# First keys of the next batch before the channel table, wide scores reordered, first norms on GpSimd

## The chip, the core and the metric

The kernel runs on one core of a Trainium2 chip. Its engines are TensorE (matmul and transpose), VectorE and ScalarE (elementwise work), GpSimd (elementwise work too) and SyncE, which here only issues DMAs. Each engine runs its own instructions in order, and engines wait for each other through semaphores. The metric is the device time of one execution in microseconds (us). Times inside an execution come from a profiled one, whose span is 833.5 us; they count from the start of that span.

## The reference

```python
def _attn_ref(q, k, v):                       # (4, 8, 768, 64)
    k_sum = k.reshape(B, H, nb, 32, D).max(axis=3)      # one key per block of 32
    v_sum = v.reshape(B, H, nb, 32, D).mean(axis=3)
    scores_l = q @ k^T / sqrt(D), kept where |i - j| < 16
    scores_s = q @ k_sum^T / sqrt(D) + log(32)
    a = softmax over both together
    return a @ [v, v_sum]

def _moe_ref(x, w_ch1, w_ch2):                # x: (4, 768, 512)
    X = np.fft.fft(np.fft.fft(x, axis=1), axis=2)
    u = x + np.real(X)
    un = (u - mean(u)) / sqrt(var(u) + 1e-06)           # over the 512 channels
    return u + np.maximum(un @ w_ch1, 0) @ w_ch2        # 512 -> 2048 -> 512
```

Four batches pass through a local attention, a real 2-D Fourier mix, a norm and a two-layer product. The weights come as 64-bit floats and are converted on the chip while the first batch is worked on ("words" in the code and the profile).

## The kernel before

The first batch's attention is written in "wide" form, two heads of a pair at a time, in four pairs (`NP = 4`); later batches use another form, which is interleaved with the dense work of the batch before by a scheduler. In the opening, the order on TensorE and VectorE is the program's own order; the DMA order is the program's too.

```python
def block_sums(b, gg):                # sums of the values over blocks of 32, for four heads
    ...
    for i in range(4):
        fetch(out=raw[i], in_=src[:, n * i:n * (i + 1)])
    add = gtt if done_weights else tt         # GpSimd once the weights are done, VectorE before
    add(raw[0], raw[0], raw[1], ADD)
    add(raw[2], raw[2], raw[3], ADD)
    add(raw[0], raw[0], raw[2], ADD)
    if not done_weights:
        nc.vector.tensor_reduce(out=vb, in_=raw[0]..., op=ADD, axis=AX.X)
    ...

def wide_scores(b, g, between=None):
    for half in range(2):
        n0, n1 = ...
        ps = [abank([P, NQ // 2, QB], ...) for e in range(2)]
        for n in range(n0, n1):
            for e in range(2):                # near keys
                nc.tensor.matmul(ps[e][0:WK, n - n0, :], kt[rows, ...], qt[rows, ...])
        for e in range(2):                    # block maxima of the keys, from VectorE
            nc.tensor.matmul(ps[e][WK:P], km[rows, :], qt[rows, QB * n0:QB * n1])
        for e in range(2):
            nc.scalar.activation(out=p[:, e, n0:n1], in_=ps[e], func=AF.Exp, scale=SC)
            tt(p[:, e, n0:n1], p[:, e, n0:n1], wide[...], ALU.mult)      # mask
        if half == 0 and between:
            between()                         # the value sums of the first or second four heads

def first_attention():
    p = {0: wide_scores(0, 0, lambda: add_blocks(0))}
    prepare(0, 1)                             # transposes of queries and keys, maxima km
    sum_values(0, 0)
    load(0, 3)
    for g in range(NP - 1):
        p[g + 1] = wide_scores(0, g + 1, (lambda: add_blocks(1)) if g == 1 else None)
        wide_values(0, g, p[g], x)            # av: weights times values, reciprocal, product
        load_values(*following(0, g, 2))
        for par in range(2):
            fold_sequence(par, g)             # even and odd halves for the Fourier step
        if g == 0:
            get_tables(0)                     # fs (sequence tables) and fd (channel table)
        if g < NP - 2:
            prepare(0, g + 2)
            sum_values(0, g + 1)
        if g == NP - 3:
            load_raw(1)                       # a piece of the weights
            load(1, 0)                        # keys and queries of the next batch
            load_raw(2)
            sum_values(0, g + 2)
    fold_halves(0, 0)
    wide_values(0, NP - 1, p[NP - 1], x)
    ...                                       # the last fold steps

def gen_fourier(b):
    ...   # y: product with fs;  mx: product with fd, added to x;  then the norm, per half
        y, z = norm[:, 0], norm[:, 1]
        if b == 0:
            nc.vector.tensor_scalar(out=minus, in0=both[:, :, 0], scalar1=-1.0, ...)
            nc.vector.tensor_scalar(out=var, in0=both[:, :, 1], scalar1=1e-6, ...)
        ...
        nc.vector.tensor_scalar(out=y (int32), in0=var (int32), scalar1=1, op0=arith_shift_right)
        nc.vector.tensor_scalar(out=y (int32), in0=y, scalar1=-1.0, scalar2=float(0x5F3759DF), ...)
        for _ in range(3):                    # Newton steps for 1/sqrt
            nc.vector.scalar_tensor_tensor(out=z, in0=y, scalar=-0.5, in1=y, op0=mult, op1=mult)
            tt(z, z, var, ALU.mult)
            nc.vector.scalar_tensor_tensor(out=y, in0=z, scalar=1.5, in1=y, op0=ADD, op1=mult)
        ins = nc.vector.tensor_tensor(out=z, in0=minus, in1=y, op=mult)
    ...   # un = x * y + z (VectorE and ScalarE), transposed by TensorE (unt) and copied to u,
          # then four sums of u; the hidden layer (hx, hy, hz) reads u

block_sums(1, 0)                              # after first_attention: values of the next batch
```

Of the kernel before, what the change touches and what calls it, by code (L numbers as in the profile page):

```python
# [487 lines left out]
def _main_program(ctx, tc, q, k, v, moe_w_ch1, moe_w_ch2, out):  # L488
# [95 lines left out]

    def add_blocks(gg):
        raw, vb = to_add[gg]
        n = BLOCK * D // 2
        while n > D:
            tt(raw[:, 0:n], raw[:, 0:n], raw[:, n:2 * n], ADD)
            n //= 2  # L590
        tt(vb, raw[:, 0:D], raw[:, D:2 * D], ADD)

    def block_sums(b, gg):

        heads, rows = slice(4 * gg, 4 * gg + 4), 4 * nb
        f = BLOCK // 4
        n = f * D
        vb = spool.tile([rows, D], FP, tag="vbs", bufs=2, name=f"vbs_{b}_{gg}")
        for g in (2 * gg, 2 * gg + 1):
            sums[b, g] = vb, sel[:, g % 2]  # L600
        src = v[b, heads].rearrange("h (n f) d -> (h n) (f d)", f=BLOCK)
        if b == 0:

            raw = words[0:rows, 4 * n * gg:4 * n * (gg + 1)]
            fetch(out=raw, in_=src)
            to_add[gg] = raw, vb
            return
        if done_weights:
            raw = room(f"vb_{b}_{gg}")
            raw = [raw[0:rows, n * i:n * (i + 1)] for i in range(4)]  # L610
        else:

            raw = [bpool.tile([P, NC, P], FP, tag="s", bufs=5, name=f"vb_{b}_{gg}_{i}").rearrange("p n t -> p (n t)")
                   [0:rows] for i in range(4)]
        for i in range(4):
            fetch(out=raw[i], in_=src[:, n * i:n * (i + 1)])

        add = gtt if done_weights else tt
        add(raw[0], raw[0], raw[1], ADD)
        add(raw[2], raw[2], raw[3], ADD)  # L620
        add(raw[0], raw[0], raw[2], ADD)
        if not done_weights:
            nc.vector.tensor_reduce(out=vb, in_=raw[0].rearrange("p (f d) -> p d f", d=D), op=ADD, axis=AX.X)
        else:
            while f > 2:
                f //= 2
                gtt(raw[0][:, 0:f * D], raw[0][:, 0:f * D], raw[0][:, f * D:2 * f * D], ADD)
            gtt(vb, raw[0][:, 0:D], raw[0][:, D:2 * D], ADD)

# [72 lines left out]
    def wide_scores(b, g, between=None):  # L704

        kt, km, qt = kt_bufs[g % 2], km_bufs[g % 2], nat[b, g]
        p = apool.tile([P, 2, NQ, QB], FP, tag="p", name=f"p_{b}_{g}")
        for half in range(2):
            n0, n1 = NQ // 2 * half, NQ // 2 * (half + 1)
            ps = [abank([P, NQ // 2, QB], f"sc_{b}_{g}_{half}_{e}") for e in range(2)]  # L710
            for n in range(n0, n1):
                for e in range(2):
                    rows = slice(D * e, D * (e + 1))
                    nc.tensor.matmul(ps[e][0:WK, n - n0, :], kt[rows, QB * n:QB * n + WK],
                                     qt[rows, QB * n:QB * (n + 1)], start=True, stop=True)
            for e in range(2):
                rows = slice(D * e, D * (e + 1))
                nc.tensor.matmul(ps[e][WK:P], km[rows, :], qt[rows, QB * n0:QB * n1], start=True, stop=True)
            for e in range(2):
                nc.scalar.activation(out=p[:, e, n0:n1], in_=ps[e], func=AF.Exp, scale=SC)  # L720
                tt(p[:, e, n0:n1], p[:, e, n0:n1], wide[:, None, :].to_broadcast([P, NQ // 2, QB]), ALU.mult)
            if half == 0 and between:
                between()
        return p

    def sum_values(b, g):

        ps = abank([P, 2, D], f"vs_{b}_{g}")
        for e in range(2):
            vb, pick = sums[b, g]  # L730
            nc.tensor.matmul(ps[WK:P, e], pick[:, D * e:D * e + 32], vb, start=True, stop=True)

        (nc.vector.tensor_copy if g in (0, NP - 1) else nc.scalar.copy)(
            out=wide_vw(g)[WK:P, :, :, 0:D], in_=ps[WK:P, :, None, :].to_broadcast([P - WK, 2, NQ, D]))

    def wide_values(b, g, p, x):
        vw = wide_vw(g)
        av = [abank([P, NST, D1], f"av_{b}_{g}_{e}") for e in range(2)]
        for n in range(NQ):
            for e in range(2):  # L740
                nc.tensor.matmul(av[e][QB * (n % 2):QB * (n % 2 + 1), n // 2, :], p[:, e, n, :], vw[:, e, n, :],
                                       start=True, stop=True)
        for e in range(2):
            rc = rec[:, b * NP + g, e]
            nc.vector.reciprocal(out=rc, in_=av[e][:, :, D])
            tt(x[:, :, P * g + D * e:P * g + D * (e + 1)], av[e][:, :, 0:D],
               rc[:, :, None].to_broadcast([P, NST, D]), ALU.mult)
# [63 lines left out]
    def first_attention():  # L811

        x = x_of[0] = bpool.tile([P, NST, DM], FP, tag="x", bufs=2, name="x_0")
        fold = bpool.tile([P, 7, 2, S2], FP, tag="u", name="fold_0").rearrange("p a k n -> p (a k n)")
        wt["fold"] = fold[:, 0:3 * HT * DM].rearrange("p (i t d) -> p i t d", i=3, t=HT)
        p = {0: wide_scores(0, 0, lambda: add_blocks(0))}
        prepare(0, 1)
# [4 lines that stand above are left out]
            wide_values(0, g, p[g], x)  # L822
            load_values(*following(0, g, 2))
            for par in range(2):
                fold_sequence(par, g)
            if g == 0:
                get_tables(0)
            if g < NP - 2:
                prepare(0, g + 2)
                sum_values(0, g + 1)  # L830
            if g == NP - 3:
                load_raw(1)
                load(1, 0)
                load_raw(2)
                sum_values(0, g + 2)
        fold_halves(0, 0)
        wide_values(0, NP - 1, p[NP - 1], x)
        for par in range(2):
            fold_sequence(par, NP - 1)
            if par:  # L840
                fold_halves(par, 0)
            fold_halves(par, 1)
            fold_ends(0, par, wt["fold"][:, par], wt["fold"][:, 2 - 2 * par])
# [160 lines left out]
    def get_tables(b):  # L1004
        tag, bufs = ("w1", 3) if b else ("w2", NC)
        fs = []
        for par in range(2):
            t = bpool.tile([P, 2, HT, F2 + 1], FP, tag=tag, bufs=bufs, name=f"fs_{b}_{par}")
            fetch(out=t, in_=dr["fs"].ap()[par])
            fs.append(t)  # L1010
        if b:
            fd = bpool.tile([P, C["fm"].shape[1]], FP, tag=tag, bufs=bufs, name=f"fm_{b}")
            fetch(out=fd, in_=dr["fm"].ap())
        else:
            fd = bpool.tile([P, 6, HD], FP, tag=tag, bufs=bufs, name=f"fd_{b}")
            fetch(out=fd, in_=dr["fd"].ap())
        tables[b] = fs, fd
        return fs, fd

    def mix_halves(ps, y, fm, xt, half):  # L1020

# [16 lines left out]
    def gen_fourier(b):  # L1038
        x = x_of[b]
        Q = DM // 4  # L1040
        fs, fd = tables[b] if b in tables else get_tables(b)


        bank = abank if b else dense_bank
# [40 lines left out]
        for half in range(2):  # L1085
# [5 lines left out]
            for i in range(HT):  # L1091
# [23 lines left out]
                                     accum_out=var[:, i:i + 1])  # L1115
                yield

            y, z = norm[:, 0], norm[:, 1]
            if b == 0:
                nc.vector.tensor_scalar(out=minus, in0=both[:, :, 0], scalar1=-1.0, scalar2=None, op0=ALU.mult)  # L1120
                nc.vector.tensor_scalar(out=var, in0=both[:, :, 1], scalar1=1e-6, scalar2=None, op0=ADD)
            else:
                nc.vector.tensor_scalar(out=var, in0=var, scalar1=1.0 / DM, scalar2=1e-6, op0=ALU.mult, op1=ADD)
            nc.vector.tensor_scalar(out=y.bitcast(I32), in0=var.bitcast(I32), scalar1=1, scalar2=None,
                                    op0=ALU.arith_shift_right)
            nc.vector.tensor_scalar(out=y.bitcast(I32), in0=y.bitcast(I32), scalar1=-1.0, scalar2=float(0x5F3759DF),
                                    op0=ALU.mult, op1=ADD)
            for _ in range(3):
                nc.vector.scalar_tensor_tensor(out=z, in0=y, scalar=-0.5, in1=y, op0=ALU.mult, op1=ALU.mult)
                tt(z, z, var, ALU.mult)  # L1130
                nc.vector.scalar_tensor_tensor(out=y, in0=z, scalar=1.5, in1=y, op0=ADD, op1=ALU.mult)
            ins = nc.vector.tensor_tensor(out=z, in0=minus, in1=y, op=ALU.mult)
            if b == 0:
                marks["mx", 0] = ins.ins
            norms.append((y, z))
# [191 lines left out]
    nc.vector.memset(vs, 0.0)  # L1327
    nc.vector.tensor_scalar(out=vs[:, :, D], in0=half_of, scalar1=float(BLOCK), scalar2=None, op0=ALU.mult)

    block_sums(1, 0)  # L1330

    def second_attention():
        prepare(1, 0)
# [76 lines left out]
```

## Time and profile before

| | |
|---|---|
| time, median of 3 runs | 838.29 us (837.83 to 839.15) |
| span of the profiled execution | 833.5 us |
| TensorE busy | 803.7 us (96%), 6074 matmuls |
| VectorE busy | 487.5 us (58%), 1117 instructions |
| ScalarE busy | 254.9 us (31%) |
| GpSimd busy | 16.1 us (2%), 27 instructions |
| moved by DMA | 120.55 MB, mean 145 GB/s |

In the profile, a row of the timeline has its start and length in us, the engine, the line of the kernel, the operation, what it writes and reads, the shape and the count; square brackets give how long the engine had been idle and what ended that. `PE` is TensorE, `DVE` VectorE, `ACT` ScalarE, `POOL` GpSimd, `SPq` the queue in which SyncE issues DMAs. A row of waits has the total, the number and the longest. A matmul of 32-bit floats is recorded several times. Line 562 is a helper for elementwise operations, so the names of the tiles tell which one is meant.

### The profile page before, as it was taken

The numbers are of one execution on the slowest core, as the hardware profiler recorded it, in microseconds if no ns is written. First come the engines' busy times: TensorE is split into PE (matmuls) and PEld (weight loads), VectorE is DVE, ScalarE is ACT, GpSimd is POOL, SyncE is SP. The second block draws the span as 40 slices with busy tenths as digits, with TensorE's granted clock in tenths as the row PEclk, the third lists the DMA queues.
The fourth block names the chain that finished last, engine by engine and source line by source line (L and its number), as shares of the span: only waits on it lengthen the run. The fifth ranks groups of instructions, "written<-read, shape, count | busy, mean of one in ns | idle before, by whom it ended". The sixth has DMA issues, their size and how long they took to land.

```text
span 833.5 us, 14698 instructions
## 1 busy us (share of the span) xinstructions
PE 803.7 (96%) x6074; PEld 577.3 (69%) x6074; DVE 487.5 (58%) x1117; ACT 254.9 (31%) x561; POOL 16.1 (2%) x27
## 2 busy tenths in 40 slices
PE   8978998999999999999999999999999999999997
PEld 5757655445578855886568875787667875786586
DVE  5778998977978553543376823542357833532351
ACT  3543756444635023203234213121323502101200
POOL 0010000000000200020000000000000000000000
PEclk9989999999999999999999999999999999999999
DMA  9997697978733277247443253423312235205001
GB/s 227 216 252 146 193 246 253 289 244 259 241 108 110 83 268 200 83 77 254 101 92 103 82 208 122 127 38 131 121 46 89 71 108 209 89 1 220 1 26 54
DMA packets 101612, 120.55 MB, mean 145 GB/s; under 512 B 50560, under 2 KB 83552, under 8 KB 101344
## 3 DMA queue, kind: packets, MB, share of 16 engines
q1 hardware_dynamic: 100848, 119.31, 48.6%
q8 instruction: 50, 0.82, 0.4%
q10 hardware_dynamic: 688, 0.20, 0.1%
q14 instruction: 26, 0.21, 0.1%
HBM read 96.96 MB, written 22.54 MB: 143 GB/s over the span
## 4 chain that ended last, share of the span: by engine, by line
PE 83%; DVE 10%; ACT 3%; issue 1%; DMA 1%; ACTq 0%; DVEq 0%
PE hx L1173 18%; PE ox L1237 17%; PE hz L1173 9%; PE oz L1237 8%; PE y L1072 4%; PE o L1214 4%; PE hy L1173 4%; PE oy L1237 4%; PE mx L1029 2%; PE sc L757 2%; DVE x L562 1%; PE unt L1151 1%; PE y L1076 1%; ACT qt L696 1%; PE av L790 1%
## 5 line engine op out<-in xcount | busy, mean ns | idle before, releaser
L1173 PE MATMUL hx<-u,w 128*128 128x384 f32 x512 | 186.2, 491 | 7.2 <-DVE h L562 3.3
L1173 PEld LDWEIGHTS hx<-u,w 128*128 128x128 f32 x512 | 94.5, 190 | 72.1 <-DVE h L562 7.0
L1173 PE MATMUL hz<-u,w 128*128 128x384 f32 x256 | 93.3, 487 | 0.0
L1237 PE MATMUL ox<-w,s 128*128 128x256 f32 x336 | 81.5, 381 | 0.3
L1237 PE MATMUL oz<-w,s 128*128 128x256 f32 x336 | 80.7, 379 | 0.0
L1237 PE MATMUL ox<-w,h 128*128 128x256 f32 x336 | 78.4, 381 | 0.4 <-DVE x L562 0.4
L1173 PEld LDWEIGHTS hz<-u,w 128*128 128x128 f32 x256 | 48.4, 190 | 34.3 <-ACT h L1190 1.1
L562 DVE TENSOR_TENSOR x<-ox,x 128x256 f32<-128x256 f32 x84 | 35.3, 421 | 62.1 <-PE ox L1237 62.0
L1237 PEld LDWEIGHTS ox<-w,h 128*128 128x128 f32 x336 | 63.2, 190 | 11.1 <-DVE x L562 1.5
L1237 PEld LDWEIGHTS oz<-w,s 128*128 128x128 f32 x336 | 63.5, 190 | 8.4
L1237 PEld LDWEIGHTS ox<-w,s 128*128 128x128 f32 x336 | 62.5, 190 | 9.2 <-DVE x L562 1.1
L562 DVE TENSOR_TENSOR h<-hx,h 128x384 f32<-128x384 f32 x32 | 17.7, 555 | 67.4 <-PE hx L1173 67.4
L1183 ACT COPY h<-hx 128x384 f32<-128x384 f32 x32 | 15.3, 477 | 127.3 <-PE hx L1173 115.6
L562 DVE TENSOR_TENSOR h<-hy,h 128x384 f32<-128x384 f32 x32 | 17.8, 556 | 60.6 <-PE hy L1173 57.4
L1173 PE MATMUL hy<-u,w 128*128 128x384 f32 x128 | 46.6, 487 | 0.0
L1214 PE MATMUL o<-w,h 128*128 128x512 f32 x96 | 42.6, 596 | 1.2 <-DVE w L562 1.2
L1237 PE MATMUL oy<-w,h 128*128 128x256 f32 x168 | 39.8, 379 | 0.0
L1199 ACT ACTIVATE h<-hx 128x384 f32<-128x384 f32 x32 | 15.7, 489 | 78.7 <-PE hx L1173 78.6
L1072 PE MATMUL y<-fs,fold 128*128 128x193 f32 x192 | 37.9, 344 | 0.1
L1072 PEld LDWEIGHTS y<-fs,fold 128*128 128x128 f32 x192 | 32.1, 195 | 6.3 <-issue 4.9
L1173 PEld LDWEIGHTS hy<-u,w 128*128 128x128 f32 x128 | 24.2, 190 | 17.1 <-DVE w L562 0.6
L1237 PEld LDWEIGHTS oy<-w,h 128*128 128x128 f32 x168 | 31.9, 190 | 4.3
(141 smaller groups left out, 1073.2 us busy)
## 6 DMA issues: line engine op xcount, KB each, us to landing
w<-dw SPq DMA_DIRECT2D x44, 896.0 KB, 5.1
words<-in_moe_w_ch_dram SPq DMA_DIRECT2D x32, 512.0 KB, 6.6
dw<-w SPq DMA_DIRECT2D x12, 896.0 KB, 6.8
vw<-in_v_dram SPq DMA_DIRECT2D x47, 192.0 KB, 5.2
kn<-in_k_dram SPq DMA_DIRECT2D x16, 384.0 KB, 4.5
qn<-in_q_dram SPq DMA_DIRECT2D x16, 384.0 KB, 5.1
out_dram<-x SPq DMA_DIRECT2D x24, 256.0 KB, 2.0
fs<-c_fs SPq DMA_DIRECT2D x8, 579.0 KB, 3.5
```

Source lines behind the costliest of these rows:

```text
L562: nc.vector.tensor_tensor(out=out, in0=in0, in1=in1, op=op)
L696: nc.scalar.copy(out=dst[D * e:D * (e + 1), s:S:2], in_=ps[D * s:D * (s + 1)])
L757: nc.tensor.matmul(ps[h][r:r + 64, i, :], kt[rows, o:o + 64], qt[rows, o:o + BLOCK], start=True, stop=True)
L790: nc.tensor.matmul(av[r][32 * j:32 * (j + 1), t, :], p[rows, h, i - NB2 * h, :], vw[rows, i, :], start=(t == 0), stop=False, skip_group_ch ...
L1029: nc.tensor.matmul(out, y[:, g], table, start=True, stop=last, skip_group_check=True)
L1072: nc.tensor.matmul(y, fgs[par][:, st, P * g:P * (g + 1)], fs[par][:, g % 2, st, :], start=(st == 0), stop=(st == HT - 1))
L1076: nc.tensor.matmul(ps[0:1, par:par + F2 + 1], zq[:, par, s2:s2 + 1], fs[par][:, 0, s2, :], start=False, stop=False, skip_group_check=True)
L1173: nc.tensor.matmul(ps, w[:, a, kk, :], u[:, r, kk, :], start=start and kk == 0, stop=stop and kk == 1, skip_group_check=True)
L1183: nc.scalar.copy(out=c11, in_=X)
L1199: nc.scalar.activation(out=c21, in_=X, func=AF.Relu)
L1214: nc.tensor.matmul(ps, h[:, n, hf, P * t:P * (t + 1)], wt[2, b, j][:, 2 * hf:2 * hf + 2, :], start=(n, hf) == (0, 0), stop=(n, hf) == (NC ...
L1237: nc.tensor.matmul(ps, left[a][:, n, :], wt[2, b, j][:, r, :], start=start and n == 0, stop=stop and n == NC - 1, skip_group_check=True)
```

## The change

It has four parts. The next batch's first keys and queries, two pieces of the weights and the values for the next batch's block sums are loaded ahead of the channel table, which is wanted only after y; the additions of those values are called apart from their load, and end in two additions instead of a reduce. The wide scores do the near keys of both halves before the key maxima of either, so that TensorE has work while VectorE makes the maxima; they use all four attention banks of PSUM at once, and the values move to the other four banks. The first batch's norms run on GpSimd, but for the shift, to leave VectorE to other work. For this a Newton step is written with four simple instructions instead of three, which holds for the later batches' norms on VectorE too.

```diff
     def add_blocks(gg):
         raw, vb = to_add[gg]
-        n = BLOCK * D // 2
-        while n > D:
-            tt(raw[:, 0:n], raw[:, 0:n], raw[:, n:2 * n], ADD)
+        n = BLOCK * D
+        add = gtt if done_weights else tt
+        if isinstance(raw, list):
+            add(raw[0], raw[0], raw[1], ADD)
+            add(raw[2], raw[2], raw[3], ADD)
+            add(raw[0], raw[0], raw[2], ADD)
+            raw, n = raw[0], n // 4
+        while n > 2 * D:
             n //= 2
-        tt(vb, raw[:, 0:D], raw[:, D:2 * D], ADD)
+            add(raw[:, 0:n], raw[:, 0:n], raw[:, n:2 * n], ADD)
+        add(vb, raw[:, 0:D], raw[:, D:2 * D], ADD)
...
-    def block_sums(b, gg):
+    def block_sums(b, gg, now=True):
...                                  # the additions go out of it
+        to_add[2] = raw, vb
+        if now:
+            add_blocks(2)
...                                  # wide_scores
+        ps = [[abank([P, NQ // 2, QB], ...) for e in range(2)] for half in range(2)]
+        for n in range(NQ):
+            half, i = divmod(n, NQ // 2)
+            for e in range(2):
+                nc.tensor.matmul(ps[half][e][0:WK, i, :], kt[rows, ...], qt[rows, ...])
         for half in range(2):
-            ps = [abank(...) for e in range(2)]
-            for n in range(n0, n1):
-                for e in range(2):
-                    nc.tensor.matmul(ps[e][0:WK, n - n0, :], kt[rows, ...], qt[rows, ...])
             for e in range(2):
-                nc.tensor.matmul(ps[e][WK:P], km[rows, :], qt[rows, QB * n0:QB * n1])
+                nc.tensor.matmul(ps[half][e][WK:P], km[rows, :], qt[rows, QB * n0:QB * n1])
...                                  # sum_values, wide_values
-        ps = abank([P, 2, D], f"vs_{b}_{g}")
+        ps = bank([P, 2, D], f"vs_{b}_{g}")
-        av = [abank([P, NST, D1], f"av_{b}_{g}_{e}") for e in range(2)]
+        av = [bank([P, NST, D1], f"av_{b}_{g}_{e}") for e in range(2)]
...                                  # first_attention; get_tables(0) no longer loads fd
             if g == 0:
                 get_tables(0)
+            elif g == 1:
+                load(1, 0)
+                load_raw(2)
+                block_sums(1, 0, False)
+                get_channel_table(0)
...
             if g == NP - 3:
-                load_raw(1)
-                load(1, 0)
-                load_raw(2)
                 sum_values(0, g + 2)
...                                  # gen_fourier
+            eng = nc.vector if b else nc.gpsimd
...                                  # the scalings, the step and the last product: eng
             for _ in range(3):
-                nc.vector.scalar_tensor_tensor(out=z, in0=y, scalar=-0.5, in1=y, op0=mult, op1=mult)
-                tt(z, z, var, ALU.mult)
-                nc.vector.scalar_tensor_tensor(out=y, in0=z, scalar=1.5, in1=y, op0=ADD, op1=mult)
+                eng.tensor_tensor(out=z, in0=y, in1=y, op=ALU.mult)
+                eng.tensor_tensor(out=z, in0=z, in1=var, op=ALU.mult)
+                eng.tensor_scalar(out=z, in0=z, scalar1=-0.5, scalar2=1.5, op0=mult, op1=ADD)
+                eng.tensor_tensor(out=y, in0=y, in1=z, op=ALU.mult)
...
-    block_sums(1, 0)
+    add_blocks(2)
```

The scheduler that orders the dense stages answers to these durations. In the changed program, three of the first batch's transposes of un stand on TensorE before the first values product of the next batch's attention, and the other three after its first sixth; VectorE adds the new block sums right after the folds; and in later batches one or two matmuls of the batch before move ahead of the transposes of un.

## The prediction

> **What bounds the kernel now.** I read the busy slices of the page first, then the table of stages, then the timeline of the stages where TensorE is not full, and last the waits.
>
> ```profile
> ## 2 busy tenths in 40 slices
> PE   8978998999999999999999999999999999999997
> DVE  5778998977978553543376823542357833532351
> PEclk9989999999999999999999999999999999999999
> ```
>
> Each digit is 20.8 us. TensorE is full nearly everywhere, VectorE only in the first ten slices. The table of stages (columns: TensorE, weight loads, VectorE, ScalarE, GpSimd busy us with counts, granted clock, DMA share, GB/s) says how much TensorE leaves idle in each:
>
> ```profile
> 0.00:52.00 52.00, 41.68 (x642) 31.35 (x642) 36.51 (x83) 21.30 (x42) 2.80 (x13) 0.97 0.99 224
> 52.00:75.50 23.50, 23.50 (x111) 18.81 (x110) 15.83 (x39) 7.34 (x22) 1.97 (x3) 0.91 0.95 208
> 75.50:91.00 15.50, 12.97 (x346) 10.87 (x346) 14.68 (x52) 11.52 (x21) 0.00 (x0) 0.89 0.63 164
> 91.00:130.00 39.00, 34.96 (x321) 21.19 (x321) 38.76 (x80) 25.75 (x52) 0.00 (x0) 1.00 0.86 230
> 200.00:834.00 634.00, 621.78 (x4173) 459.52 (x4171) 321.69 (x745) 156.75 (x369) 11.30 (x12) 1.00 0.37 118
> ```
>
> 10.3 us idle before 52, none from 52 to 75.5, 2.5 to 91, 4.0 to 130 with VectorE full, 12.2 spread over the last 634. The change touches little after 130 us, so it plays for the first three gaps, 16.8 us, of which most belongs to work it leaves alone. Behind 130 TensorE is a queue: what it gains earlier arrives at the end unshortened.
>
> The end of the opening, in the timeline:
>
> ```profile
> 42.05 0.50 SPq L549 DMA_DIRECT2D kn<-in_k_dram  x1
> 42.59 0.54 SPq L549 DMA_DIRECT2D qn<-in_q_dram  x1
> 47.47 0.85 PE L694 MATMUL qk<-ident,kn 128*128 128x128 f32 x6 [3.02 <-DMA kn<-in_k_dram]
> 49.62 0.55 DVE L873 TENSOR_TENSOR fold<-fold 128x381 f32<-128x381 f32 x1
> 49.74 1.51 PE L694 MATMUL qk<-ident,qn 128*128 128x128 f32 x6 [1.42 <-DVE fold L562]
> 51.77 0.42 PE L757 MATMUL sc<-qt,kt 64*64 64x32 f32 x2 [0.52 <-ACT qt L696]
> 52.12 2.94 PE L1072 MATMUL y<-fs,fold 128*128 128x193 f32 x8
> ```
>
> The first Fourier product y stands in TensorE's queue behind the transposes of the next batch's first keys and queries and two score matmuls. Those keys were issued at 42.05 and landed 5.3 us later; the queries took 7.0 us from 42.59, to 49.6, which is when their transposes start (the release named, a fold step, only comes last by a hair). y's own input, the even half of the fold, is ready at 50.17. So the next batch's load costs y 1.95 us.
>
> Further on, TensorE's waits from 75 to 130 us:
>
> ```profile
> PE hx L1173 <- DVE h L562: 2.3, 1, 2.3
> PE vs L780 <- DVE norm L1126: 1.8, 1, 1.8
> ```
>
> The second is really the sums of values (a reduce that ends at 81.0), which queue on VectorE between the Newton steps. The first norms take VectorE from 73.95 to 86.33: 28 instructions of 0.15 us, 4.2 us, stretched because each step of three numbers per partition waits its turn behind 0.7 us instructions.
>
> **What the Trainium skill says.** GPSIMD Engine Reference, 3.1 Elementwise — side-by-side cycle accounting: about 2.6 cycles an element for two inputs plus a software dispatch per instruction. Three elements are all dispatch. The trace has such sizes, by form:
>
> ```profile
> L868 POOL COPY zq<-fold 128x3 f32<-128x3 f32 x2 | 1.0, 490 | 2.3 <-DVE fold L562 2.3
> L565 POOL TENSOR_TENSOR vbs<-vb 96x64 f32<-96x64 f32 x2 | 0.6, 316 | 128.9 <-PE vs L780 128.9
> L1294 POOL COPY vw<-wide 128x24 f32<-128x24 f32 x2 | 0.4, 228 | 5.1 <-DMA wide<-c_count 5.1
> ```
>
> A 128x24 copy beside an idle VectorE takes 0.23 us, a 128x3 copy beside VectorE's adds 0.49. That agrees with SBUF — State Buffer, Who interferes with whom: a VectorE instruction with two SBUF inputs and a GpSimd instruction that reads SBUF exclude each other; one 128x6 copy here lasted 1.33 us beside such adds (51.70). TensorE: Matmul & The Clock Gate, Part 1: The HAM clock gate, says that an idle window of about 3.4 us halves the clock and a busy one restores it. The trace agrees: the clock reads 0.50 from about 49.4 to 56.0, after the thin stretch from 44.5, and again from 83.4 to 86.4 after the wait at 79.3. So a gap removed or made costs up to 1.7 us besides itself.
>
> **Part 1, wide scores.** No instruction is added; per head pair the 24 near-key matmuls of the second half (1.24 us) go ahead of the key-maximum ones (0.8). For pair 0 that fills TensorE's 1.5 us wait for the maximum, for nothing: VectorE is full and its order is kept. For pair 1 the first half's scores come 1.24 us later, VectorE starts its mask about 0.65 us later (20.4 for 19.76), but the 1.16 us it waits before the second half vanishes. I walked the queues forward with durations from the timeline (near keys 1.23 a half, maxima 0.77, av 1.6, transposes 2.62, mask pair 1.03): av of pair 0 ends at 22.2 for 22.99; pair 2's first mask starts at 29.0 for 28.53 (a loss); pair 3's second mask ends at 40.9 for 41.73. All that follows on VectorE moves 0.85 us: even fold ready at 49.3. The values now share four PSUM banks with the transposes; I find waits of 0.15 us there and neglect them.
>
> **Part 2, load order.** Ahead of the keys stood the channel table (768 KB) and one 512 KB piece of weights. From 31.7 to 49.6 the queue moved about 3.85 MB, some 0.22 to 0.24 MB per us; 1.3 MB less is 5.5 us. Keys land near 42, queries near 44.5, transposes run at once after the last av (42.6), eight ScalarE copies of 0.52 us end by 49, eight score matmuls follow by 49.2. y then starts at 49.4 instead of 52.12: **2.7 us**, of which 0.85 are part 1's. The table is wanted at 62.5; issued near 48, with 7.9 us to landing before, it comes in time. The value sums move into VectorE's 4.9 us wait at 55.7 (four loads landed by about 53), so their 3.0 us leave the tight stretch.
>
> **Part 3, norms on GpSimd.** Per half: two scalings, one shift that stays on VectorE, one step, three Newton rounds of four, one product: 14 dependent GpSimd instructions after the shift. At 0.23 to 0.32 plus 0.08 between (from the chain of value adds on GpSimd), with some blocking, 0.35 each: 4.9 us. Statistics of half one are ready at 70.8 (73.45 less 2.7). GpSimd scalings and shift end at 71.6, the norm at 76.5 against 81.68. Then half two, whose statistics stand behind the first normalised block on VectorE, starts at 77.2 and ends at 82.6 against 86.33. So the left factor u is complete some 4.7 us earlier, at about 86 for 90.8.
>
> TensorE doesn't get all that. Its order now puts three of the un-transposes before the first pair's av, and the last three before five sixths of it. It will wait about 1.3 us near 76 and 3 us near 80, then owes av work worth 2.2 us. At an equal amount of work done it is only **1.6 us** ahead. VectorE, which limits TensorE from 91 to 130, starts the sums of u 4.7 us earlier but with 2.1 us of weight conversion less behind it: ahead by about **3 us** including the 26 small steps it no longer does. TensorE can turn 4 us of idle time there into progress, so I take VectorE's 3.0.
>
> **Part 4, later batches.** Newton has four instructions a round instead of three, 18 more of 0.15 us, and in the interleaved order of VectorE each can cost a turn. Fillers stand ahead of the un-transposes (waits there are 0.4 us in all now), so 0 to 1 us is lost; I take 0.4. The value adds of later sums in place of reduces (1.01 us each against about 0.85) bring 0.3.
>
> Sum: 3.0 + 0.3 - 0.4 = 2.9, and 0.4 for the chance that one of the two half-clock windows falls away (one in four, 1.7 us): 3.3. 838.3 - 3.3 = **835.0 us**.
>
> **Rivals.** (a) GpSimd is slow beside VectorE: 0.5 us or more a step, as the 128x3 copies are. Norm one then ends at 78.8, norm two near 88, later than now, with VectorE and TensorE both waiting in order behind it: the 2.7 us are given back, 837 to 840. For it: the measured 0.49. Against: in that stretch half of VectorE's work reads PSUM or a single SBUF input. (b) All lead survives and VectorE's unloading shows in full, with no half clock: 2.7 + 4 us of idle + 1.7, so 830. For it: VectorE at 99% and TensorE idle 4 us from 91 to 130. Against: TensorE's new order. (c) The keys come early but y waits for the fold or for ScalarE's copies: part 2 brings only 1 us; 836.5.
>
> **Range and chances.** 831 to 838.8 holds (c), most of (b) and the mild form of (a). 2% is 16.8 us, as much as all the idle time the change could reach, and no part can lose as much. Faster by over 2% 0.01, within 2% 0.98, slower 0.01.
>
> **What would show it.** y's first matmul near 49.4 with no wait of TensorE for the keys; the first mask of pair 2 a little later than now and the last of pair 3 0.8 us earlier; GpSimd's norm steps near 0.3 us, the first un-transpose near 77, the fourth near 83; the first product of the hidden layer 2 to 5 us earlier; and the same lead at 130 and at 800 us. I am wrong if GpSimd's chain lasts over 7 us, if y does not start before 51, or if the lead is lost between 90 and 130.

## The result: slower by half a per cent, and the profile after

The changed kernel takes 842.17 us, median of four runs (841.09 to 842.39), against 838.06 (836.52 to 839.15) of the kernel before: 1.0048 of it, interval 1.003 to 1.0066. The prediction had 835.0 and a range up to 838.8. So about 4 us were lost where 3.3 were to be won.

The profiled execution has a span of 840.6 us. Its busy slices, 21.0 us each:

```profile
PE   8988999999989999999999999999999999999997
PEclk9999799999989999999999999999999999999999
```

Two slices show a lowered TensorE clock, the fifth (84 to 105 us) and the twelfth (231 to 252); the second is also thin for TensorE. The record of the clock changes in steps of 3.41 us, and a step at 0.50 is called a half-clock step from here on. In the kernel before neither place stood out. The stretches of the table of stages (TensorE, weight loads, VectorE, ScalarE, GpSimd busy us with counts, granted clock, DMA share, GB/s):

```profile
75.50:91.00 15.50, 13.34 (x216) 10.81 (x213) 11.37 (x19) 9.44 (x17) 2.61 (x13) 0.68 0.76 203
91.00:130.00 39.00, 37.13 (x342) 20.77 (x341) 31.93 (x73) 21.92 (x43) 0.00 (x0) 0.95 0.57 173
200.00:834.00 634.00, 624.63 (x4171) 460.28 (x4170) 327.51 (x770) 159.71 (x372) 11.64 (x12) 0.99 0.38 120
```

From 75.5 to 91 the clock is 0.68 for 0.89, and TensorE gets through 216 matmul records for 346. From 91 to 130 VectorE is busy 31.9 of 39 us for 38.8: it is no longer full. From 200 to 834 TensorE is busier than before (624.6 us for 621.8), at a clock of 0.99, and still isn't through.

The opening did what it should. TensorE in the timeline after:

```profile
43.65 0.85 PE L692 MATMUL qk<-ident,kn 128*128 128x128 f32 x6 [0.64 <-DMA kn<-in_k_dram]
44.97 0.85 PE L692 MATMUL qk<-ident,qn 128*128 128x128 f32 x6 [0.48 <-DMA qn<-in_q_dram]
48.72 1.58 PE L1080 MATMUL y<-fs,fold 128*128 128x193 f32 x8
```

The keys' transposes are 3.8 us earlier, the queries' 4.8, y 3.4. Then the un-transposes (TensorE's transposes of the normalised un of the first batch) and the near scores (products with the neighbouring keys) of the second batch:

```profile
74.92 1.47 PE L1162 MATMUL unt<-ident,big 128*128 128x128 f32 x12
77.09 0.75 PE L789 MATMUL av<-vw,p 64*32 64x65 f32 x34
80.00 1.96 PE L1162 MATMUL unt<-ident,big 128*128 128x128 f32 x12 [2.16 <-ACT big L1155]
81.89 1.55 PE L789 MATMUL av<-vw,p 64*32 64x65 f32 x62
83.36 2.77 PE L756 MATMUL sc<-qt,kt 64*64 64x32 f32 x48
86.06 2.93 PE L1184 MATMUL hx<-u,w 128*128 128x384 f32 x4
88.92 2.77 PE L756 MATMUL sc<-qt,kt 64*64 64x32 f32 x48
```

The near scores in the kernel before, and the two exponentials of ScalarE that follow them in the changed kernel:

```profile
89.18 1.60 PE L757 MATMUL sc<-qt,kt 64*64 64x32 f32 x96
86.18 0.49 ACT L762 ACTIVATE p<-sc 128x384 f32<-128x384 f32 x1 [1.06 <-PE sc L756]
91.74 0.49 ACT L762 ACTIVATE p<-sc 128x384 f32<-128x384 f32 x1 [2.18 <-PE sc L756]
```

The first three un-transposes come 8 us earlier than before, the last three wait 2.16 us for the second norm (in the name of the ScalarE product that needs it). They stand after a third of the values product (34 of its 96 records), not after a sixth. After this thin stretch the clock record reads 0.50 from 81.0 to 94.6, four half-clock steps; before, one there.

The near scores of the next pair are 96 matmul records, for two heads and two halves of the sequence, and each half has its own bank of PSUM. Before, they ran in one group of 1.60 us. Now they run as two groups of 48, 2.77 us each at half clock. Each group is one half: the exponential of a half needs both of its heads, and one follows each group. (Some of the expectations below take the groups for the two row groups of the array, one for each head; the exponentials show that this was misread.) In the trace the 96 records start four at a time, 5 to 8 ns apart, and the 48 two at a time.

And what VectorE waits for from 75 to 130 us:

```profile
DVE words L937 <- ACT words L933: 6.2, 1, 6.2
```

The 6.2 us are a step of the weight conversion, which waits for ScalarE; ScalarE stands in its order behind the exponentials of the late scores (its own step comes at 95.16, after the exponential at 94.77). Before, VectorE waited 0.9 us in all in this stretch.

To follow a lead through the program, I matched each matmul of a trace with the same one of the trace before and took the difference of their starts (the median over some 4 us); likewise each of the 32 converted weight pieces on VectorE. Minus is ahead of the kernel before, in us:

| profiled run | TensorE near 65 | near 205 | near 245 | near 305 | 7th weight piece (108) | last piece (227) |
|---|---|---|---|---|---|---|
| changed kernel | -5.2 | -0.3 | +4.5 | +7.7 | +6.2 | +6.1 |
| E1 parts 1 and 2 | -2.6 | -4.3 | -1.8 | +1.6 | -1.3 | -0.5 |
| E4 part 2 | -3.4 | -3.0 | -0.4 | +3.5 | +0.1 | +0.9 |
| E3 later Newton of three | -2.5 | -2.7 | +1.8 | +4.7 | +3.8 | +3.8 |
| E5 parts 1, 2, outputs ahead | -2.4 | -4.1 | -1.3 | -1.5 | -1.1 | -0.4 |
| E6 changed, outputs ahead | -4.1 | -2.8 | +1.0 | +0.1 | +3.7 | +3.5 |
| E15 all three remedies | -3.9 | -6.3 | -2.1 | -2.7 | -0.1 | +0.3 |

One profile is one execution: the first column moves by 2 us with the landing of the opening's loads, and half-clock steps move the others. The medians decide; the table says where.

### The profile page after: what moved, and what is told of

Same layout as the page of the kernel before. It is cut to its first block, busy times and chain, and to the rows that moved or that the text cites. A ratio compares the mean times of both kernels' runs of the same rounds, so it can differ in the third digit from the quotient of the medians.

```text
span 840.6 us, 14727 instructions
## 1 busy us (share of the span) xinstructions
PE 810.0 (96%) x6074; PEld 578.4 (69%) x6074; DVE 487.6 (58%) x1117; ACT 255.9 (30%) x561; POOL 23.6 (3%) x59
## 3 DMA queue, kind: packets, MB, share of 16 engines
q1 hardware_dynamic: 100848, 119.31, 47.9%
## 4 chain that ended last, share of the span: by engine, by line
PE 85%; DVE 8%; ACT 4%; issue 1%; POOL 1%; DVEq 0%; POOLq 0%
PE hx L1184 19%; PE ox L1248 17%; PE hz L1184 9%; PE oz L1248 9%; PE y L1080 4%; PE hy L1184 4%; PE o L1225 4%; PE oy L1248 4%; PE sc L756 2%; PE mx L1035 2%; ACT qt L694 1%; PE unt L1162 1%; DVE x L562 1%; PE av L789 1%; PE y L1084 1%
## 5 line engine op out<-in xcount | busy, mean ns | idle before, releaser
L1184 PE MATMUL hx<-u,w 128*128 128x384 f32 x512 | 188.1, 495 | 8.4 <-ACT h L1199 3.5
```

Of the source, the lines that this page charges most:

```text
L1184: nc.tensor.matmul(ps, w[:, a, kk, :], u[:, r, kk, :], start=start and kk == 0, stop=stop and kk == 1, skip_group_check=True)
```

## Experiments

Each time below is a ratio to the kernel before, run on the same chip beside it, whose medians there were 836.0 to 836.9; 0.001 is 0.84 us. Theory T1 came from the traces above: the norms on GpSimd start the loss. T2: the loads do. T3: the later batches' longer Newton rounds do.

### First: which part costs

**E1, parts 1 and 2.** The third part undone:

```diff
-            eng = nc.vector if b else nc.gpsimd
+            # every norm step on nc.vector, three instructions a Newton round, as before
```

> The changed kernel with its third part undone: all norms on VectorE as in the kernel before, three instructions a Newton round; load order and wide scores stay changed. Theory T1 (the norms on GpSimd start the loss: normalised values come early, the near scores of the second batch's second pair run one row group at a time at half clock, ScalarE's queue delays the weight conversion, the conversion ends 6 us late and the second batch's first Fourier product waits for its fold): about 834 to 836 us against 838 before, TensorE about 5 us ahead at 60 to 75 us and some 2 to 4 us of it left at the end, last weight piece not later than before, no wait of more than 1 us for the fold at 240 us. Rival T2 (the earlier loads or the value sums in VectorE's wait start the debt): 841 to 843 us, last weight piece 5 to 7 us late, fold wait of about 3 us at 240. Rival T3 (the later batches' four-instruction Newton costs): about 836 to 839, and the difference to the changed kernel arises after 250 us.

0.9997 (0.9982 to 1.0013). T2 falls: parts 1 and 2 aren't slower. But T1 expected 2 to 4 us left at the end, and nothing is left.

**E2, part 3 alone** on the kernel before.

> The kernel before with the third part alone: first norms on GpSimd, four instructions a Newton round in the later batches; loads and wide scores as before. T1: slower than before, 840 to 843 us, with the near scores of the second batch's second pair split by row group, the last weight piece 4 to 7 us late and the wait for the second batch's fold as in the changed kernel. T2: 836 to 838.5 us, weight pieces on time. T3: 838.5 to 840, with the loss after 250 us and none at 240.

1.0106 (1.0073 to 1.014), in six runs that reach from 840.6 to 849.5. The norms part is slower by itself, without the new loads and scores; T3's loss after 250 us alone doesn't fit, for the last weight piece is 4.6 us late at 227. The 8.9 us are twice what the same part costs on top of parts 1 and 2 (4.3 us, E1 to the changed kernel), so the parts don't simply add. In its trace the wait for the second norm is 3.53 us (2.16 in the changed kernel), y waits 2.8 us for the fold near 238, and the mean clocks of its six runs give 7.0 half-clock steps a run for 4.8 in the kernel before. What each of these is worth was not separated.

**E3, later Newton rounds of three** in the changed kernel:

```diff
             for _ in range(3):
+                if b:
+                    ... the three VectorE instructions of before; continue
                 eng.tensor_tensor(out=z, in0=y, in1=y, op=ALU.mult)
```

> The changed kernel, but the later batches' Newton rounds have three instructions again; the first batch's norms stay on GpSimd. T1: 841 to 842.5 us, within 1 us of the changed kernel, same late weight pieces. T3 (the 18 more small instructions of the later batches cost a turn of VectorE each): 837 to 839 us, with the lag gone after 250 us.

1.0045 (1.0023 to 1.0067), as the changed kernel: T3 falls. In its trace the clock reads 1.00 from 75 to 100 us, and the weight pieces are 3.8 us late all the same: the four half-clock steps of the changed kernel's profile are not needed for that.

**E4, part 2 alone.**

> The kernel before with the second part alone: the next batch's first keys ahead of the channel table, value sums later; norms and scores as before. T1: 835 to 837 us, y's first matmul near 49.5 us, a lead of about 3 us at 75 and of 1 to 3 us at the end. T2: 840 to 843 us, last weight piece late and a wait for the second batch's fold at 240. If y stands before the last output tile of the first batch in TensorE's queue and this alone is the cause (T5), there is a wait for the fold of 2 us or more at 240 here too though the weight pieces are on time.

1.0019 (1.0002 to 1.0036). Neither T1's gain nor T2's loss: weight pieces on time, y at 49.30, and yet nothing won. Its trace and E1's say where. Timeline of TensorE in E1:

```profile
228.00 1.89 PE L1245 MATMUL oy<-w,h 128*128 128x256 f32 x8
232.77 1.22 PE L1080 MATMUL y<-fs,fold 128*128 128x193 f32 x6 [2.88 <-DVE fold L562]
234.79 0.60 PE L1080 MATMUL y<-fs,fold 128*128 128x193 f32 x2 [0.80 <-DVE fold L562]
```

and in the kernel before:

```profile
234.15 1.89 PE L1237 MATMUL oz<-w,s 128*128 128x256 f32 x8
236.18 1.22 PE L1072 MATMUL y<-fs,fold 128*128 128x193 f32 x6
```

This is the second batch's first Fourier product. VectorE in the kernel before, and then in E1:

```profile
230.75 0.69 DVE L562 TENSOR_TENSOR s<-h 128x512 f32<-128x512 f32 x1 [0.59 <-ACT h L1180]
231.36 1.75 DVE L562 TENSOR_TENSOR fold<-x 128x1536 f32<-128x1536 f32 x1
228.20 1.76 DVE L562 TENSOR_TENSOR fold<-x 128x1536 f32<-128x1536 f32 x1
236.36 0.69 DVE L562 TENSOR_TENSOR s<-h 128x512 f32<-128x512 f32 x1
```

In E1 TensorE has ended oy at 229.9 and finds the fold not ready. The output matmuls oz, which stood ahead of y before, now stand behind it. They need a sum s of VectorE, which before came ahead of the fold and now comes after it. The fold starts 3.2 us earlier than before, but TensorE, without oz in front of y, is there earlier still. So it waits 3.7 us for the lack of one sum of 0.7 us, and a half-clock step follows. From 205 to 305 us E1 loses 6 us, E4 6.4, the changed kernel 8.0 (it waits 3.4 us, with two half-clock steps at 238 to 244.8):

```profile
239.41 2.96 PE L1080 MATMUL y<-fs,fold 128*128 128x193 f32 x8 [3.37 <-DVE fold L562]
```

### Second: the order at that place (T5), and the un-transposes

**E5**: E1 with output matmuls put ahead again by precedence, one sum on VectorE and three products of TensorE:

```diff
-            tt(left[S1], a21, left[A22], ADD)
+            with ahead():     # tc.high_priority(700) for the first tile of (0, 1) only
+                tt(left[S1], a21, left[A22], ADD)
...
-            product(Z, S1, T1, True, False)
+            with ahead():
+                product(Z, S1, T1, True, False)
```

The first products X and Y of that tile are wrapped alike.

> Parts one and two of the change (norms on VectorE as before), and in TensorE's queue 12 to 16 output matmuls of the first batch (the first tile's third product, which needs one sum of VectorE, and the second tile's first) stand ahead of the second batch's first Fourier product, as they do in the kernel before; the hidden layer is as in the run of parts one and two, which was 4.5 us ahead at 225 us and had lost it by 290, with 3.7 us of waits for the fold and one half-clock window at 232 to 238. Theory T5 (TensorE arrives at the second batch's Fourier product before VectorE's fold, with nothing else in its queue, and there the whole lead goes): wait for the fold under 1.5 us, no half-clock window, a lead of 3 to 4 us kept behind 290, 831.5 to 834 us where the kernel before has 836. Rival T6 (VectorE alone sets that time, and work moved ahead of the wait is only missing later): still 835 to 836.5, with waits of the same length elsewhere in 240 to 300.

0.9966 (0.9953 to 0.9979), 833.21 us: faster than both kernels. TensorE in its timeline:

```profile
232.19 1.99 PE L1251 MATMUL oz<-w,s 128*128 128x256 f32 x8 [1.17 <-DVE s L562]
234.60 1.22 PE L1080 MATMUL y<-fs,fold 128*128 128x193 f32 x6
```

y itself is later than in E1 (232.77), but the wait is filled, and no half-clock step stands there. T5 holds. The lead kept near 305 is 1.5 us, not the expected 3 to 4: VectorE, for whose sum s TensorE waits 1.2 us here, is hardly ahead of the kernel before (0.4 us at the last weight piece).

**E6**: the changed kernel with the same edit.

> The changed kernel with the same 16 output matmuls ahead of the second batch's first Fourier product and nothing else altered. T5: the wait of 3.4 us for the fold falls below 1.5 and the two half-clock windows at 238 to 245 go, so 3.5 to 5 us less than the changed kernel: 836 to 837.5 on a chip where the kernel before has 836. The loss at 80 to 100 us (late weight pieces, half clock) stays, so it does not get below 835. T6: 839 to 840.5, as the changed kernel.

1.0015 (0.9995 to 1.0034) for 1.0048: 2.8 us back, as E1 to E5 (2.6). T5 holds here too, and 4.1 us remain against E5. One half of the near scores can be read here at full clock:

```profile
84.40 1.59 PE L756 MATMUL sc<-qt,kt 64*64 64x32 f32 x48 [0.67 <-ACT qt L694]
```

48 records take 1.59 us, where the kernel before ran 96 in 1.60.

**E7**: the changed kernel, un-transposes late, norms still on GpSimd:

```diff
-    drive((gen_fourier(0), 4, 600), ...)
+    # after 14 steps, from the second half's norm on: precedence 60 in place of 600
```

> The changed kernel, but from the second half's norm on the first batch's un-transposes have almost no precedence (60 places in the program's order in place of 600), so that TensorE does the values of the second batch's first pair before un-transposes three to six, and near scores of the next pair alternate between the row groups again; the norms stay on GpSimd. T1 (what costs at 80 to 100 us is TensorE's order, with its wait for GpSimd's second norm and the split near scores at half clock): half-clock windows at 81 to 95 fall from four to at most one, TensorE lags no more than 0 to 1 us at 100 to 120 where the changed kernel lags 4.3, weight pieces 12 to 31 are 2 to 5 us earlier than in the changed kernel, time 836 to 838.5. If the GpSimd norms cost through VectorE or ScalarE and not through TensorE's order, pieces stay 6 us late and the time stays at 839 to 840.5.

1.0041 (1.0023 to 1.0058). No measurable gain, against T1. But TensorE at 205 us is 3.5 ahead, 64 of the near scores' 96 records run in one group again (1.14 us), and one half-clock step is left at 85 to 95; and then y waits 3.8 us for the fold, with a clock of 0.84 from 228 to 250. What is won early is lost at the same place as in E1.

**E8**: both edits.

> The changed kernel with both: un-transposes later, and output matmuls ahead of the second batch's first Fourier product. T1 and T5 together: 832 to 835 us, below the kernel before with its 836. If the two losses are one (the late weight conversion alone), no better than the better one of the two.

0.9987 (0.9977 to 0.9998). With the wait filled the late un-transposes are worth 2.3 us (1.0015 to 0.9987). 1.8 us remain against E5.

### Third: is it VectorE's work?

Three kernels leave out one step of the weight conversion: the low word of each weight isn't added. In all three oz stands ahead of y without the edit of E5, so they are compared with the kernel before, E5 and E6.

```diff
-        nc.vector.scalar_tensor_tensor(out=tmp[:, 1, :], in0=low, scalar=2.0 ** -52, in1=tmp[:, 1, :],
-                                       op0=ALU.mult, op1=ALU.add)
```

> The kernel before with one VectorE step of the weight conversion left out: the low word of each weight isn't added (32 instructions of 0.68 us, 22 us of VectorE between 60 and 228 us; the weights keep 20 bits of mantissa). All three of these runs have output matmuls ahead of the second batch's first Fourier product, so they differ by the change alone. All theories: last weight piece at least 3 us earlier than in the kernel before, no wait for the fold at 236 us, 833 to 836 us where the kernel before has 836.

> Parts one and two of the change with the same step left out. Theory D (the lead of these parts was eaten because VectorE, with the weight conversion, did not keep up with TensorE): 4 to 5 us under the light kernel before, the lead of TensorE at 60 us still there at 300. Rival: a lead lost for another reason, 0 to 2 us under it.

> The changed kernel with the same step left out; near scores of the second batch's second pair still one row group at a time, norms on GpSimd. Theory D (what the norms on GpSimd cost is the 6 us by which the weight conversion is late): within 1.5 us of the light parts one and two, last weight piece within 1 us of theirs. Rival E (it costs TensorE's own waits and half-clock windows at 75 to 95 us, which are never made up): 3 to 5 us above the light parts one and two, the lag arising before 100 us and constant after it.

E9 0.9951 (0.9936 to 0.9966), E10 0.9907 (0.9881 to 0.9933), E11 1.0009 (0.9994 to 1.0025). E10 (six runs) is 3.7 us under E9, between the 4 to 5 of theory D and the 0 to 2 of its rival. Near 205 us it is 8.7 us ahead of the kernel before where E9 is 3.3, near 305 6.2 where E9 is 3.4: with a lighter VectorE about half of the first two parts' lead comes through. E11 contradicts theory D flatly: with 22 us of VectorE work gone it is 8.5 us above E10 (more than the 3 to 5 of rival E, too), and its last weight piece is still 5.4 us late. The same cut is worth 4.1 us in the kernel before and 4.9 in parts 1 and 2 (E5 to E10), but only 0.5 with the norms on GpSimd (E6 to E11, inside the intervals). The stretch from 75.5 to 130 us of E10:

```profile
75.50:130.00 54.50, 51.29 (x606) 31.94 (x600) 50.14 (x124) 40.83 (x80) 0.00 (x0) 1.00 0.82 217
```

and of E11:

```profile
75.50:130.00 54.50, 47.92 (x571) 30.50 (x564) 42.51 (x93) 33.27 (x65) 5.03 (x23) 0.97 0.64 177
```

VectorE is busy 42.5 us for 50.1, ScalarE 33.3 for 40.8, TensorE 47.9 for 51.3: with norms on GpSimd all three idle more. So it isn't the amount of VectorE's work; the queues wait for one another. That is rival E, with two corrections. Its half-clock steps are not needed: E11's clock reads 1.00 from 75 to 100 us. And its loss wasn't all there by 100 us: E11 is about 4 us behind E10 at 95, 7.5 at 205 and 9 near 305.

### Last: what is left of the norms' cost

**E12**: E6 with two Newton rounds in place of three in the first batch (less precise), which shortens GpSimd's chain; TensorE's order is the same.

```diff
-            for _ in range(3):
+            for _ in range(3 if b else 2):
```

> The changed kernel with the 16 output matmuls ahead (it took 1.0015 of the kernel before), and two Newton rounds in place of three in the first batch's norms: eight GpSimd instructions of about 0.27 us less, 1.1 us a half, at the price of precision; TensorE's order is the same. Theory G (the length of GpSimd's chain makes TensorE wait 2.2 us at 77.8 for the second norm, and this with the half clock after it is most of what the norms on GpSimd cost): the wait falls under 0.7 us, the second norm ends near 77 in place of 79, 2 to 4 us less, 0.997 to 0.9995 of the kernel before. Rival H (TensorE's and VectorE's order, fixed from early readiness, costs whatever the chain's length): the wait goes, but the time stays at 1.000 to 1.002.

0.9984 (0.9965 to 1.0004) for 1.0015: 2.6 us, as theory G has it, though the two intervals just overlap. TensorE's waits from 60 to 130 us in E6:

```profile
PE unt L1162 <- ACT big L1155: 2.2, 1, 2.2
PE qk L692 <- ACT p L762: 1.5, 1, 1.5
```

and in E12:

```profile
PE unt L1162 <- ACT big L1155: 1.8, 1, 1.8
PE qk L692 <- ACT p L762: 0.4, 1, 0.4
```

1.5 us of waits are gone, but less of it from the second norm's wait than expected (0.7 was the limit): counted from the first norm instruction, TensorE comes to this place 1.1 us sooner, too.

**E13**: E8 with later Newton rounds of three.

> The run with un-transposes later and output matmuls ahead (0.9987 of the kernel before), with three-instruction Newton rounds in the later batches again. If the four-instruction rounds on VectorE are the 1.8 us by which it is behind parts one and two with the same output order (0.9966): 0.9960 to 0.9972. If they cost the 0.4 us of the prediction or nothing: 0.998 to 0.999.

0.9985 (0.9968 to 1.0002), as E8. The longer rounds cost nothing measurable, the second time.

**E14**: part 1 alone.

> The kernel before with the first part alone, wide scores with the near keys of both halves first. The prediction had 0.85 us for it by the fold: y's first matmul does not move by that alone (it waits for the keys), so 0 to 0.9 us, 0.999 to 1.0005 of the kernel before. Output matmuls stand ahead of the second batch's first Fourier product as in the kernel before.

0.9998 (0.9981 to 1.0014): nothing by itself.

**E15**: E8 with two Newton rounds in the first batch.

> The changed kernel with un-transposes later, output matmuls ahead, and two Newton rounds in place of three in the first batch's norms on GpSimd (less precision). If the length of GpSimd's chain is also the rest of what the norms on GpSimd cost (1.8 us between 0.9987 and the 0.9966 of parts one and two): 0.996 to 0.9975. If a later un-transpose has already hidden the chain: 0.998 to 0.999, as without it.

0.9971 (0.9954 to 0.9988), against E5's 0.9966: with outputs ahead, un-transposes late and a shorter chain the norms on GpSimd cost nothing measurable. E8 to E15 is 1.3 us, with overlapping intervals.

**E16**: part 2 alone with outputs ahead.

> The kernel before with the second part alone and the output matmuls ahead of the second batch's first Fourier product. If the first part brings nothing once the order at that place is kept: 0.996 to 0.9975, as parts one and two together (0.9966). If it brings the 0.85 us of the prediction: 0.9973 to 0.9985.

0.9983 (0.9963 to 1.0003). The edit is worth 3.0 us here (E4 1.0019). Beside part 2, part 1 may be worth 1.4 us (E5 0.9966), not resolved.

## Why the prediction was wrong

**The opening: right in its sum, not in its shares.** y was to start at 49.4; in the 14 profiles with early loads it starts at 48.25 to 50.35, mean 49.2; in three of the four with late loads at 51.6 to 52.2, in the fourth (E14) at 54.8. Against the mean of those three that is 2.8 us for the predicted 2.7. But E4 and E16, which lack part 1, start y at 49.30 and 49.06: the 0.85 us that I gave part 1 don't show there. I had also read y's input half a us too late in the kernel before: in the changed kernel y starts at 48.72, while the fold step that I took for its input runs to 49.08. Pair 2's first mask comes at 28.70 (29.0 predicted); pair 3's last ends at 40.65 (40.9).

**GpSimd's chain: right.** 0.35 us a step was a little much (0.19 to 0.44 long, mostly 0.28 from start to start), 4.9 us for a norm close: 68.30 to 73.1 and 73.86 to 79.1, 4.8 and 5.2 us. Rival (a), a slow GpSimd, did not happen, though the time landed beyond its range. Of the two waits that I foresaw, the one near 80 us is there (2.16 us for 3). The 1.5 us near 74 aren't the other: there the next keys' transposes wait for an exponential, and the first un-transposes wait for nothing. The hidden layer's first product is 4.7 us earlier (86.06 for 90.72), as I had it, but it now stands between the two groups of near scores.

**"At an equal amount of work done it is only 1.6 us ahead": wrong.** Near 105 us TensorE is about 3.5 us behind, in E3 and E6, whose programs are the same up to there, about 1 (rough figures, since the orders differ there). With this my own sign of being wrong came true: the lead was lost between 90 and 130. I counted waits and work owed. I left out that the owed work would run slower: near scores split by halves take twice the time (1.59 us for 48 records). Half-clock steps come on top, as many as an execution happens to get: from 78 to 98 us four in the profile of the changed kernel, two in E2, one each in E6 and E12, none in E3 and E11. I had given half clock 0.4 us as a gain, and 1.7 us as its most, though my own trace read 0.50 for two steps on end.

**"I take VectorE's 3.0": wrong.** The 26 small steps went, and VectorE waited for ScalarE instead (6.2 us once); its seventh weight piece is 3.7 to 6.2 us late (E3, E6, the changed kernel), not 3 early. I took a queue that is 99% busy for one whose removed work becomes progress. It is one while the norms stay on VectorE (E9, E10). With them on GpSimd it isn't: in E11 VectorE has 22 us less work and is as late.

**"Behind 130 TensorE is a queue: what it gains earlier arrives at the end unshortened": wrong, and the step that failed most plainly.** Up to 205 us the lead of E1 survives (4.3 us), as I had it; then it meets VectorE, which ends the weight conversion only 0.5 us earlier than before and only then folds the second batch. The kernel before hides this with output matmuls in front of y, and the scheduler, given the new timing, put y first. Four pairs that differ by this order agree: 2.6 us (E1, E5), 2.8 (changed, E6), 3.0 (E4, E16), 4.5 (E7, E8). The prediction weighs the order between 75 and 130 us and not at 230, which nothing in the diff touches. Even with the order kept, E5 loses 2.6 us of lead from 205 to 305 us.

**Part 4: a cost of 0.4 us**: not measurable, twice (1.0045 for 1.0048, 0.9985 for 0.9987).

The sum, in ratios: parts 1 and 2 with the order kept -2.8 us (E5); the order at 232 us +2.6; the norms on GpSimd +4.3 (E1 to the changed kernel). Of these 4.3, with the wait at y filled, the un-transposes' place gives back 2.3 (E6 to E8), and the chain's length a further 1.3 (E8 to E15), after which 0.4 against E5 is inside the intervals. This sum holds for norms added last; E2's 8.9 us for the norms alone are not explained by it. That the earlier readiness of un drew its transposes forward is read in the two orders. Why the scheduler then split the near scores by halves (one of the two PSUM banks may have been held longer) was not shown. Nor was the path from TensorE's lateness over ScalarE's order to the late weight pieces: no run changed ScalarE's order alone.

## What to carry to other kernels

Where a scheduler fixes each engine's order from estimated readiness, a change that makes one thing ready earlier reorders places far from it: compare the whole order of the engine that bounds, and look for every place where it meets a second engine with nothing else queued. In these runs a lead reached the end only as far as the slower partner of the next meeting had it too, or other work was put in front of the wait; here precedence for three output products and one sum turned a lost lead into 2.6 us, and parts 1 and 2 with them are the best version measured without leaving work out (833.21 us, 0.9966 of the kernel before). Taking work off a busy engine can give nothing if its remaining instructions wait in order for another's: 22 us off VectorE gave 4.9 us in one order and 0.5 in the other.

## What the runs showed that I had not expected

TensorE's half clock can outlast a busy stretch. The Trainium skill, TensorE: Matmul & The Clock Gate, Part 1: The HAM clock gate, has one busy window restore full speed; in the kernel before the record agrees (one step at 83.3 after the thin stretch from 80.1). In the changed kernel TensorE is recorded busy 3.40 of every 3.40 us from 81.2 on, and the clock still stays at 0.50 for four steps. The measurement decides, with one reserve: the ends of matmuls in a trace are modelled. What counts as busy for the clock stays open.

Half-clock steps also go with much of the scatter between executions: over the 22 runs of E5, with the number of steps worked out from each run's mean clock, the time rises 1.4 us a step (correlation 0.88); over the 60 runs of the kernel before beside them 1.2 (0.76). Their mean number was 5.8 in the changed kernel (four runs), 4.7 in the kernel before, 3.4 in E5. In the nine runs of E3, as slow as the changed kernel, it was 4.2: the loss doesn't need them.

Near scores gain a factor of two when both halves run together: 96 records in 1.60 us against 48 in 1.59 at the same clock. Each matmul has 64 rows and 64 columns, and two heads times two halves take four places in the array. The skill's Part 3: Packing small matmuls — row/col tiling, on the same page, says that matmuls which fill only part of the array can run in it at once, each at its own tile position. The starts in the traces agree with it: four within 20 ns and the next four 59 ns after the first, against two within 7 ns and the next two again 59 ns after.
